# Dealing out the last row-maximum tiles: a fixed five in every projection stretch, the rest in the first three blocks of the last visits

## The chip, the cores and the metric

The kernel runs on one core of one Trainium2 chip. The metric is device time in microseconds (us), lower is better. Before the change the median of three runs is 1620.94 us (1620.45 to 1621.42).

## The reference, cut to what matters

```python
# x: (1, 2048, 640); 32 heads of 20; one key and one value head shared by all query heads
g = sigmoid((x * gate_w).sum(-1, keepdims=True))
q = (x @ wq) -> (1, 32, 2048, 20);  k = x @ wk;  v = x @ wv
p = softmax(einsum("bhqd,bkd->bhqk", q, k) * 20 ** -0.5)
a = einsum("bhqk,bkd->bhqd", p, v) -> (1, 2048, 640) @ wo
h = layernorm(B_x)                                  # over the 640 channels
u = gelu(einsum("bsd,sf->bdf", h, w1) + b1)         # token mixing, F = 1728
b = einsum("bdf,fs->bds", u, w2) + b2, transposed back
out = g * a + (1 - g) * b
```

Everything is float32. The softmax is exact: each row of scores has its own maximum subtracted.

## The kernel before, in words

**Units and visits.** The attention is cut into 32 units (`NU`): 4 blocks of 512 queries times 8 groups of 4 heads. A unit is visited 16 times, once for every block of 128 keys, so there are 512 visits. For one visit TensorE makes 4 score tiles (128 keys by 512 queries, one head each; `qk`, L703), ScalarE turns each into `p` with one exponential (L712), and `pv_group` (L738) multiplies the four `p` tiles by the values. Two visits are closed by one group of L738 instructions, which therefore marks the end of a stretch or block of work in the trace.

**Two row halves.** A score tile contracts only 62 rows. TensorE is used as two halves of 64 rows, called lane 0 and lane 1 here (`b` in the code), which work on different tiles at the same time. A score tile, a maximum tile and a 64-row projection matmul (320 columns) each take one lane. The group L738 takes all 128 rows, so both lanes have to be done before it.

**Row maxima.** The scores of a unit need its row maxima first. They come from extra tiles, the same products the other way round (128 queries by 512 keys, `ms_next`, L491), each followed by a VectorE maximum into one column of `mp` (L497): 32 tiles per lane and unit, 1024 per lane in all. When a unit has all of them, `ms_done` takes the maximum over four columns (VectorE, L512), GpSimd negates it and splits it in two (L514 to L516). `store_max` transposes it (VectorE, L523) and writes it to DRAM (`m_scr`, L524); `fetch_max` reads it back with four DMAs into rows 60, 61, 124 and 125 of the query tile `qst` (L531), two for each lane. A score of the next unit cannot start before its lane's two rows have landed. SyncE (SP) issues these DMAs in program order, like all others.

**Stretches.** The order of all engines' work is written out by hand while the program is built. The middle of the kernel is a list `ph` of 244 stretches. `main(k, ...)` issues one: one lane gets score tiles ("s") and maximum tiles ("m") after a letter pattern, the other one the projection matmuls ("F") and a few tiles; then come the last steps of the stretch and a group L738 for two visits. A small clock (`issue`, `bank_take`, `bank_give`, with 0.232 us for a tile and 0.147 us for an F) decides which lane issues next, and which of the PSUM banks in `pool` a tile gets. `later` is a list of small steps that close an earlier unit; `settle` takes one or two of them at fixed places.

The last 32 stretches (`4 * NA`, k from 212 to 243) are the **projection stretches**: their F are 15 matmuls by `wo` (L949) for the first 8 tiles of tokens. Their pattern holds 4 "m" for one lane and 1 for the other, and `share(k)` says how many of the maximum tiles still left a stretch makes. When all maxima are made, `spare[0]` becomes true, which among other things brings three more buffers for `p` into use.

**The last visits.** The last 26 visits (`TAIL`) are made in 13 **blocks** of two (`BLOCKS`, v = 486, 488, ... 510). A block has 8 score tiles, one visit ahead of the visits that it closes, and as its F the `wo` matmuls that are left (L904; `tail_take`). How many F a block gets follows from what its lane still has to do until the end (`own` and `tail`). In the loop a lane issues a score when enough banks are free by the clock, otherwise an F; then comes L738. The first score of the last unit (visit 496) stands in the block that begins at v = 494, the fifth. Behind the blocks comes an end of about 13 us with the last head group.

Of the kernel before, what the change touches and what calls it, by code (L numbers as in the profile page):

```python
# [27 lines left out]
NU = NQB * NQ  # L28
PRO = 7
LEAD = 46  # L30
TAIL = 26
BLOCKS = (2,) * 13
NA = 8
NP = 12
EPS = 1e-5
GC = math.sqrt(2.0 / math.pi)
# [4 lines left out]
def mix_kernel(ctx: ExitStack, tc: tile.TileContext, A_x, A_wq, A_wk, A_wv, A_wo,  # L41
               B_x, B_w1, B_b1, B_w2, B_b2, gate_w, out):
    nc = tc.nc
    x = A_x[0]
    y_out = out[0]

    def f32(ap):
        return ap.bitcast(F32)
# [25 lines left out]
    def view(t, at, n):  # L74
        return t[:, at:at + n * HD2].rearrange("p (a b) -> p a b", b=HD2)
# [84 lines left out]
    def new_qmax(n):  # L160
        if n < NU and n not in qmax:
            qmax[n] = load_q(n, "qmx")
# [9 lines left out]
    with tc.tile_pool(name="pa", bufs=1) as pa, \  # L172
# [18 lines left out]
        more = [w1r.tile([P, HS, P], F32, name="wr").rearrange("p (i j) f -> p i (j f)", i=2) for _ in range(3)]  # L191
# [255 lines left out]
    u_lo = [view(t, FC * HD2, FC) for t in (u0, slot[0])]  # L447
    pp_pool = ctx.enter_context(tc.tile_pool(name="pp", bufs=NP))
    ev = ctx.enter_context(tc.tile_pool(name="ev", bufs=1))
# [4 lines left out]
    X_US, F_US, PV_US = 0.232, 0.147, 0.858  # L454
    USE = {"exp": ("act", 0.43, 0.477, 0.65), "max": ("dve", 0.43, 0.6, 0.735), "sum": ("dve", 0.35, 0.47, 0.6)}

    def bank_take():
        i = min(range(len(pool)), key=lambda j: pool[j][0])
        return pool.pop(i)[1]

    def bank_give(bank, use):
        engine, lag, us, held = USE[use]
        start = max(clock[engine], clock["now"] + lag)
        clock[engine] = start + us
        pool.append((start + held, bank))
        return start + held

    def busy(engine, us):
        clock[engine] = max(clock[engine], clock["now"]) + us
# [3 lines left out]
    row_max = {}  # L473
    mtiles = {}
    lead_banks = [True]
    given = [0, 0]
    issued = [0, 0]

    def ms_next(b):
        k = given[b]  # L480
        if k >= 32 * NU:
            return None
        given[b] += 1
        n, r = divmod(k, 32)
        (kq, pr), qt = divmod(r // 4, 2), r % 4

        def step():
            if n not in mtiles:
                mtiles[n] = mpool.tile([P, 16, 4], F32, name="mp")
            ms = psl.tile([P, NB], F32, name="ml") if lead_banks[0] else bank_take()  # L490
            nc.tensor.matmul(ms, qmax[n][64 * b:64 * b + 60, pr, qt * P:(qt + 1) * P],  # L491
                             kst[64 * b:64 * b + 60, kq * NB:(kq + 1) * NB], start=True, stop=True)
            if not lead_banks[0]:
                bank_give(ms, "max")
            c = (2 * b + pr) * 4 + qt
            behind, last["ins"] = last["ins"], None
            r = nc.vector.tensor_reduce(mtiles[n][:, c, kq:kq + 1], ms, axis=AX.X, op=ALU.max)  # L497
            if behind is not None:
                tc.add_manual_dep(r.ins, behind.ins.name, SYNC, reason="row tiles that share a bank")
                last["sig"] = r  # L500
            issued[b] += 1
            if min(issued) == 32 * n + 1:
                new_qmax(n + 1)

        return step

    def ms_done():
        n = len(row_max)
        if n < NU and min(issued) >= 32 * (n + 1):
            mm = mmpool.tile([P, 16], F32, name="mm")  # L510
            busy("dve", 0.14)
            nc.vector.tensor_reduce(mm, mtiles.pop(n), axis=AX.X, op=ALU.max)  # L512
            mn = mmpool.tile([P, 2, 16], F32R, name="mn")
            nc.gpsimd.tensor_scalar(mm, mm, -1.0, None, op0=ALU.mult)  # L514
            nc.gpsimd.tensor_copy(mn[:, 0, :], mm)
            nc.gpsimd.tensor_sub(mn[:, 1, :], mm, f32(mn[:, 0, :]))  # L516
            row_max[n] = mn

    def store_max(n):
        mn = row_max[n]  # L520
        mt = mpool.tile([P, 32], F32, name="mt")
        busy("dve", 0.19)
        nc.vector.transpose(mt, f32(mn).rearrange("p j c -> p (j c)"))  # L523
        nc.sync.dma_start(out=m_scr[n], in_=mt)  # L524
# [139 lines left out]
    def split_wo(c):  # L664
        wr = wos[c]
        nc.gpsimd.tensor_copy(wo_hi[:, c, :], wr)
        nc.gpsimd.tensor_sub(wo_lo[:, c, :], wr, f32(wo_hi[:, c, :]))

    units = [(n, kb) for n in range(NU) for kb in range(NS)]
    ptiles = {}  # L670
    spare = [False]
    sc = [0, 0]
# [3 lines left out]
    def banks_at(t):  # L676
        return sum(e <= t for e, _ in pool)

    def next_p():
        turn_p[0] += spare[0]  # L680
        i = turn_p[0] % (NP + 3)
        return extra_p[i - 1] if 0 < i < 4 else pp_pool.tile([P, NB], F32, name="p")

    def s_next(b):
        j = sc[b]
        if j >= 2 * len(units):
            return None
        sc[b] += 1

        def step():  # L690
            qk(j // 2, j % 2, b)

        step.score = True
        return step
# [160 lines left out]
    HEAD = (H - 4) * DH  # L855
    jobs = [(st, 0, D) for st in range(NA, NS - 4)]
    jobs += [(st, 0, CUT) for st in range(NS - 4, NS)] + [(st, CUT, HEAD) for st in range(NS - 4, NS)]
# [126 lines left out]
    def split_last(raw):  # L984
        hi, lo = spare_row(0, F32R), spare_row(1, F32R)
        nc.gpsimd.tensor_copy(hi, raw)
        nc.gpsimd.tensor_sub(lo, raw, f32(hi))
        return hi, lo
# [40 lines left out]
    for i, (steps, rest, done) in enumerate(seq):  # L1029
        item, j = divmod(i + 1, 2)  # L1030
        rest.insert(0, lambda c=4 * (PRO + item) + 2 * j: w1_upto(c + 4))
    def stretches(seq):
        return [(rows[1 - b], rest if b else [], done if b else []) for rows, rest, done in seq for b in range(2)]

    ph = stretches(seq)
    m = len(ph)
# [6 lines left out]
    for c in range(DC):  # L1043
        ph[m + 18 + 16 * c][1].append(lambda c=c: load_wo(c))
        ph[m + 22 + 16 * c][1].append(lambda c=c: split_wo(c))
    aj = [a_jobs(st) for st in range(NA)]
    ph[-8][1].append(aj[0][0])
    ph += stretches(batches(aj, [1] * 2 * NA))
    visits = [0] + [2] * (len(ph) - 1)
    assert sum(visits) == len(units) - TAIL  # L1050
    early = NS - 4 - NA + 4
    for i in range(early):
# [15 lines left out]
    sent, back_in = {0}, {0}  # L1068
# [5 lines left out]
    def pattern(k):  # L1074
        return PATTERN[len(ph[k][0]) if visits[k] else 0]

    base = [[pattern(k)[int(k % 2 != h)].count("m") for k in range(len(ph))] for h in range(2)]

    def share(k):
        left = [32 * NU - x for x in given]  # L1080
        if k >= len(ph) - 4 * NA:
            return [(x * c[k] + sum(c[k:]) // 2) // sum(c[k:]) for x, c in zip(left, base)]
        over = [sum(c[k:]) - x for x, c in zip(left, base)]
        h = over.index(max(over))
        return [c[k] - (i == h and k % 4 == 1 and k < m and over[h] > 0) for i, c in enumerate(base)]

    lanes = [0.0, 0.0]
# [85 lines left out]
    v = 0  # L1173
    clock.update(now=0.0, act=0.0, dve=0.0, pv=0.0)
    for k in range(len(ph)):
        n = visits[k]
# [3 lines left out]
            raw = last_wo()  # L1180
        if k == len(ph) - 2:
            w_last = split_last(raw)
    assert v == len(units) - TAIL and spare[0]

    if NU - 1 not in sent:
        store_max(NU - 1)

    pool.append((lanes[0], ps_g.tile([P, NB], F32, name="g")))
    begin = lanes[0]
# [5 lines left out]
    for i in range(4):  # L1195
        tail_load(NS - 4 - NA + i, late=True)

    for n in BLOCKS:
        ends = [min(2 * len(units), 2 * (v + n) + 2) for _ in range(2)]
        lanes = [[], []]  # L1200
        own = [(2 * len(units) - c) * X_US for c in sc]
        while any(sc[b] < ends[b] for b in range(2)):
            b = int(sc[1] < sc[0])
            lanes[b].append(s_next(b))
        left = len(units) - v
        fs = [tail_take(b, len(tail[b]) if n == left else
                        max(0, round(((own[b] + len(tail[b]) * F_US) * n / left - len(lanes[b]) * X_US) / F_US)))
              for b in range(2)]
        at = [begin, begin]
        while any(lanes) or any(fs):  # L1210
            b = 0 if at[0] <= at[1] and (lanes[0] or fs[0]) or not (lanes[1] or fs[1]) else 1
            soon = sum(any(first for _, first in f[:3]) for f in fs)
            score = lanes[b] and (not fs[b] or banks_at(at[b]) > soon)
            if score or fs[b][0][1]:
                at[b] = max(at[b], min(e for e, _ in pool))
            clock["now"] = at[b]
            if score:
                lanes[b].pop(0)()
                at[b] += X_US
            else:  # L1220
                fs[b].pop(0)[0]()
                at[b] += F_US
        begin = max(at) + 0.38 + n * 0.927
        for _ in range(n):
            settle()
            pv_group([v], True)
            v += 1
        if NU - 1 not in back_in:
            fetch_max(NU - 1)
            back_in.add(NU - 1)  # L1230
        if v == 492:
            load_mid()
        if v >= 502 and len(loaded) < len(jobs):
            for i in range(len(loaded), len(jobs)):
                tail_load(i)
# [80 lines left out]
```

## Time and profile before

| | |
|---|---|
| median of three runs | 1620.94 us |
| the profiled execution, its own time | 1621.32 us |
| its span, from the first to the last instruction | 1619.5 us |
| TensorE clock granted | 1.000 |
| PE busy, share of the span | 1612.7 us, 100% |
| DVE (VectorE) busy | 1352.9 us, 84% |
| ACT (ScalarE) busy | 1309.9 us, 81% |
| POOL (GpSimd) busy | 867.9 us, 54% |
| projection stretches, from L738 to L738 | 1377.09 to 1534.32 us |
| the 13 blocks | 1534.32 to 1606.45 us |

Matmuls overlap and their ends are modelled, so a busy PE says only that some matmul was under way. Where TensorE time goes is read here from starts: from one group L738 to the next, and from one matmul to the next in its lane.

### The profile page before, as it was taken

The page shows a single profiled execution, that of the slowest core. Times are in us where ns is not written, and L with a number is a line of the kernel's source. Part 1 is how long each engine was busy: PE and PEld are TensorE (multiplying, and loading weights), DVE is VectorE, ACT ScalarE, POOL GpSimd, SP SyncE. Part 2 cuts the span into 40 slices and gives each one's busy share as a digit, 9 for nine tenths or more (in the row PEclk, how much of TensorE's full clock was granted, in tenths as well). Part 3 has the DMA queues.
Part 4 walks back from the last instruction along what each step waited for, and adds up shares of the span by engine and source line. Part 5 has one row for each costly group of instructions (what it writes and reads, how often), then busy time and mean ns, then how long its engine had stood idle before and what let it go on. Part 6 is the DMA issues. An engine that isn't in the chain of part 4 may idle for free.

```text
span 1619.5 us, 39566 instructions
## 1 busy us (share of the span) xinstructions
PE 1612.7 (100%) x14877; PEld 1126.8 (70%) x14877; DVE 1352.9 (84%) x2344; ACT 1309.9 (81%) x2567; POOL 867.9 (54%) x974
## 2 busy tenths in 40 slices
PE   9999999999999999999999999999999999999999
PEld 7789677777777777666666666666666666666666
DVE  6689999999999999888888888888888888667623
ACT  4445788888888888888888888888888888999975
POOL 6568667786777687644544444454544442344410
PEclk9999999999999999999999999999999999999999
DMA  7655323323332232232222221222222212336421
GB/s 214 210 163 147 75 68 80 86 75 87 80 85 72 79 85 65 65 72 81 72 69 76 54 73 52 65 72 80 73 72 72 69 52 60 95 111 187 149 81 43
DMA packets 188246, 144.51 MB, mean 89 GB/s; under 512 B 43474, under 2 KB 150127, under 8 KB 188055
## 3 DMA queue, kind: packets, MB, share of 16 engines
q1 hardware_dynamic: 187766, 141.66, 31.5%
q8 instruction: 117, 1.92, 0.5%
q14 instruction: 75, 0.61, 0.1%
q10 hardware_dynamic: 288, 0.33, 0.1%
HBM read 108.38 MB, written 32.15 MB: 87 GB/s over the span
## 4 chain that ended last, share of the span: by engine, by line
PE 99%; DVE 1%; ACT 0%; issue 0%; DVEq 0%; ACTq 0%
PE ms L738 16%; PE g L816 11%; PE s L738 10%; PE ms L703 10%; PE g L1004 9%; PE s L703 8%; PE s L491 7%; PE ms L491 6%; PE pp L299 4%; PE pu L624 3%; PE o L703 3%; PE o L738 3%; PE o L491 2%; PE g L949 2%; PE ml L491 1%; PE ms L904 1%
## 5 line engine op out<-in xcount | busy, mean ns | idle before, releaser
L497 DVE TENSOR_REDUCE mp<-s 128x1 f32<-128x512 f32 x895 | 586.4, 680 | 68.1 <-PE s L491 56.7
L712 ACT ACTIVATE p<-ms 128x512 f32<-128x512 f32 x938 | 545.3, 617 | 47.3 <-PE s L738 16.8
L497 DVE TENSOR_REDUCE mp<-ms 128x1 f32<-128x512 f32 x763 | 503.3, 680 | 69.5 <-PE ms L491 58.6
L751 POOL TENSOR_TENSOR acc<-acc,part 128x512 f32<-128x512 f32 x212 | 274.1, 1293 | 444.6 <-ACT part L750 432.8
L712 ACT ACTIVATE p<-s 128x512 f32<-128x512 f32 x818 | 480.2, 616 | 33.2 <-PE ms L738 10.7
L703 PE MATMUL ms<-qst,kst 62*128 62x512 f32 x938 | 366.5, 409 | 0.1
L491 PE MATMUL s<-kst,qmx 60*128 60x512 f32 x895 | 358.6, 415 | 0.6 <-DVE yo L547 0.5
L703 PE MATMUL s<-qst,kst 62*128 62x512 f32 x818 | 322.4, 409 | 0.2 <-ACT p L712 0.2
L1004 PE MATMUL g<-slot,wh 64*128 64x320 f32 x1344 | 306.0, 312 | 0.0
L491 PE MATMUL ms<-kst,qmx 60*128 60x512 f32 x763 | 302.4, 411 | 0.0
L738 PE MATMUL ms<-p,v_sb 128*32 128x512 f32 x2272 | 273.2, 598 | 0.0
L1004 PEld LDWEIGHTS g<-slot,wh 64*128 64x128 f32 x1344 | 216.6, 184 | 68.7 <-issue 54.5
L130 POOL TENSOR_TENSOR wl<-wr,wh 128x512 fp32r<-128x512 f32 (+1 forms) x176 | 217.9, 1238 | 29.6 <-ACT wh L127 12.7
L497 DVE TENSOR_REDUCE mp<-o 128x1 f32<-128x512 f32 x298 | 202.8, 681 | 35.2 <-PE o L491 29.0
L703 PEld LDWEIGHTS ms<-qst,kst 62*128 62x128 f32 x938 | 171.5, 185 | 61.5 <-ACT p L712 29.0
L1004 PE MATMUL g<-slot,wl 64*128 64x320 f32 x672 | 205.3, 306 | 0.0
L816 PE MATMUL g<-slot,wh 64*128 64x320 f32 x864 | 196.3, 309 | 0.0
L816 PE MATMUL g<-u,wh 64*128 64x320 f32 x864 | 196.3, 309 | 0.0
L703 PEld LDWEIGHTS s<-qst,kst 62*128 62x128 f32 x818 | 151.2, 185 | 53.7 <-ACT p L712 35.6
L712 ACT ACTIVATE p<-o 128x512 f32<-128x512 f32 x277 | 170.8, 617 | 12.5 <-PE ms L738 5.5
L738 PE MATMUL s<-p,v_sb 128*32 128x512 f32 x1424 | 171.2, 598 | 0.2 <-ACT p L712 0.2
L491 PEld LDWEIGHTS s<-kst,qmx 60*128 60x128 f32 x895 | 164.3, 185 | 5.6 <-DVE yo L547 0.7
(247 smaller groups left out, 3080.1 us busy)
## 6 DMA issues: line engine op xcount, KB each, us to landing
wr<-in_B_w_dram SPq DMA_DIRECT2D x136, 256.0 KB
qmx<-q_scr SPq DMA_DIRECT2D x192, 80.0 KB
qst<-q_scr SPq DMA_DIRECT2D x192, 80.0 KB
ot<-l_scr SPq DMA_DIRECT2D x120, 64.0 KB
y_scr<-yo SPq DMA_DIRECT2D x16, 320.0 KB
slot<-o_scr SPq DMA_DIRECT2D x16, 320.0 KB
o_scr<-ot SPq DMA_DIRECT2D x124, 40.0 KB
o_scr<-acc SPq DMA_DIRECT2D x124, 40.0 KB
```

The lines of the kernel that those rows point to most:

```text
L130: nc.gpsimd.tensor_sub(wl[:, :nv], wr[:, :nv], f32(wh[:, :nv]))
L299: nc.tensor.matmul(pp, w, t, start=first and n == 0, stop=not more and n == len(steps) - 1)
L491: nc.tensor.matmul(ms, qmax[n][64 * b:64 * b + 60, pr, qt * P:(qt + 1) * P], kst[64 * b:64 * b + 60, kq * NB:(kq + 1) * NB], start=True, s ...
L497: r = nc.vector.tensor_reduce(mtiles[n][:, c, kq:kq + 1], ms, axis=AX.X, op=ALU.max)
L624: nc.tensor.matmul(pu[r][:, :HD2], w[rows, c, :], h[rows, st, :], start=(st == 0 and k == 0), stop=(st == NS - 1 and k == 2))
L703: nc.tensor.matmul(s, kst[64 * b:64 * b + 62, kb * P:(kb + 1) * P], q[64 * b:64 * b + 62, pr, :], start=True, stop=True)
L712: e = nc.scalar.activation(p, s, AF.Exp, scale=SCALE)
L738: nc.tensor.matmul(o[32 * hh:32 * hh + 32, :], v_sb[:, kb + i, :], ptiles.pop((u, hh)), start=opened and i == 0, stop=(i == len(us) - 1) a ...
L751: nc.gpsimd.tensor_add(sums[0], sums[0], part)
L816: other_tile(half, nc.tensor.matmul(hold["p"][:, :HD2], w[r, i, :], u[d][r, fc, :], start=(hold["n"] == 1), stop=(hold["n"] == 6 * FC - 3)))
L949: other_tile(half, nc.tensor.matmul(hold["p"][:, :HD2], o[r, c, :], w[r, c, d * HD2:(d + 1) * HD2], start=(hold["n"] == 1), stop=(hold["n" ...
L1004: other_tile(half, nc.tensor.matmul(hold["p"][:, :HD2], w[r, st % HS, :], h[d][r, st, :], start=(hold["n"] == 1), stop=(hold["n"] == 6 * NS)))
```

## The change

`share` gives each projection stretch the number of its pattern, `c[k]` (4 for one lane and 1 for the other), as long as any are left, instead of a proportional part of what is left. What remains is put into the lanes of the first three blocks (`LAST_M`): each takes an equal part of it (rounded up), spread evenly between the block's scores. `own`, from which the number of F follows, counts these tiles too. `ms_done` stands behind each block, and the last unit's `store_max` and `fetch_max` stand together behind the block that makes its last maximum. `spare[0]` is set by hand where the blocks begin.

```diff
+LAST_M = 3
...
     def share(k):
         left = [32 * NU - x for x in given]
         if k >= len(ph) - 4 * NA:
-            return [(x * c[k] + sum(c[k:]) // 2) // sum(c[k:]) for x, c in zip(left, base)]
+            return [min(x, c[k]) for x, c in zip(left, base)]
...
-    assert v == len(units) - TAIL and spare[0]
-
-    if NU - 1 not in sent:
-        store_max(NU - 1)
+    assert v == len(units) - TAIL
+    spare[0] = True
...
-    for n in BLOCKS:
+    for j, n in enumerate(BLOCKS):
         ends = [min(2 * len(units), 2 * (v + n) + 2) for _ in range(2)]
         lanes = [[], []]
-        own = [(2 * len(units) - c) * X_US for c in sc]
+        own = [(2 * len(units) - c + 32 * NU - m) * X_US for c, m in zip(sc, given)]
         while any(sc[b] < ends[b] for b in range(2)):
             b = int(sc[1] < sc[0])
             lanes[b].append(s_next(b))
+        for b in range(2):
+            more = -(-(32 * NU - given[b]) // max(1, LAST_M - j))
+            for i in range(more):
+                lanes[b].insert((i + 1) * len(lanes[b]) // more, ms_next(b))
...
         begin = max(at) + 0.38 + n * 0.927
+        ms_done()
         for _ in range(n):
             settle()
             pv_group([v], True)
             v += 1
-        if NU - 1 not in back_in:
+        if NU - 1 in set(row_max) - sent:
+            store_max(NU - 1)
+            sent.add(NU - 1)
             fetch_max(NU - 1)
             back_in.add(NU - 1)
```

Line numbers of the changed kernel are higher by one up to the loop over the blocks (L491 becomes L492, L738 becomes L739).

## The prediction

> **What bounds the kernel now.** I read the chain that ended last first, because it says which engine's time can move the end.
>
> ```profile
> PE 99%; DVE 1%; ACT 0%; issue 0%; DVEq 0%; ACTq 0%
> ```
>
> TensorE carries 99% of the chain, so a change is worth what it does to the spacing of TensorE's starts. The order of instructions of the changed program shows where to look: every engine issues the same number of instructions as before, and the first one that stands elsewhere on TensorE lies in the middle of the projection stretches. So I cut the last part into windows at starts of the group L738, which closes each stretch and block: eleven stretches (k = 212 to 222), the other 21, and the 13 blocks.
>
> ```profile
> 1377.09:1429.76 52.67, 52.67 (x486) 33.67 (x485) 35.17 (x59) 51.01 (x105) 24.08 (x24) 1.00 0.33 94
> 1429.76:1534.32 104.56, 104.56 (x938) 66.43 (x937) 72.92 (x125) 99.48 (x201) 41.48 (x44) 1.00 0.53 160
> 1534.32:1606.45 72.13, 72.13 (x740) 48.90 (x739) 20.95 (x39) 52.27 (x105) 9.05 (x11) 1.00 0.18 55
> ```
>
> Columns are the window, its length, then busy time of PE, PEld, DVE, ACT and POOL, clock, DMA share and GB/s. The maximum tiles alone (line L491) in the first two windows:
>
> ```profile
> 1377.09:1429.76 52.67, 20.98 (x55) 9.29 (x55) 1.00 0.33 94
> 1429.76:1534.32 104.56, 46.36 (x118) 20.12 (x118) 1.00 0.53 160
> ```
>
> The first eleven stretches have 55 maximum tiles, five each, and take 52.67 / 11 = 4.788 us each. The next 21 have 118 = 21 x 5 + 13: thirteen of them hold a sixth tile. This is the comparison that the change needs, made by the kernel itself.
>
> **The change part by part: the stretches.** With five tiles everywhere, the 21 stretches should look like the eleven: 21 x 4.788 = 100.55 us instead of 104.56, so 4.01 us go, 0.308 us for each sixth tile. That is more than the tile's own step in its lane, which is 0.23 us here (first pair of rows), while a projection matmul F steps 0.15 us (second pair):
>
> ```profile
> 1558.37 0.39 PE L703 MATMUL o<-qst,kst 62*128 62x512 f32 x1
> 1558.60 0.39 PE L703 MATMUL g<-qst,kst 62*128 62x512 f32 x1
> ```
>
> ```profile
> 1538.96 0.31 PE L904 MATMUL g<-slot,u 64*128 64x320 f32 x1
> 1539.11 0.31 PE L904 MATMUL g<-slot,u 64*128 64x320 f32 x1
> ```
>
> The reason is in the letters: the sixth "m" is put behind the pattern, and `main` holds the last tile of the pattern's lane back until the other lane's F are gone. So it runs with the other half of the array empty, just ahead of L738.
>
> VectorE loses 13 maxima there, which is worth nothing: it is busy 72.92 of 104.56 us. The loads of the last projection job are the cover that gets thinner. They are issued here, and first used here:
>
> ```profile
> 1509.90 0.95 SPq L845 DMA_DIRECT2D slot<-o_scr  x2
> ```
>
> ```profile
> 1516.76 0.31 PE L949 MATMUL g<-slot 64*128 64x320 f32 x1
> ```
>
> They have 6.9 us. If the chain of DMAs that leads to them, from the end of an earlier unit, keeps its own pace, the five shortened stretches along it take at most 5 x 0.308 = 1.5 us from that. I cost it at nothing; should the loads take all of 6.9 us, it costs up to 1.5 us.
>
> **The blocks.** The 13 tiles come back here: 5, 4 and 4 in the first three blocks by the order of the changed program. The F matmuls they displace move to later blocks. F before, by the second count (weight loads) of each row of L904, with the length of the block ahead of it:
>
> ```profile
> 1534.32:1539.78 5.46, 3.02 (x34) 3.02 (x34) 1.00 0.26 76
> 1539.78:1545.22 5.44, 3.08 (x33) 2.96 (x32) 1.00 0.25 79
> 1545.22:1550.76 5.54, 3.18 (x35) 3.08 (x33) 1.00 0.34 87
> 1550.76:1556.18 5.42, 3.06 (x33) 2.97 (x32) 1.00 0.36 112
> 1556.18:1561.72 5.54, 3.19 (x35) 3.09 (x33) 1.00 0.35 110
> 1561.72:1567.20 5.48, 3.12 (x33) 3.02 (x32) 1.00 0.02 3
> 1567.20:1572.83 5.63, 3.20 (x35) 3.04 (x33) 1.00 0.28 89
> 1572.83:1578.42 5.59, 3.08 (x33) 2.90 (x32) 1.00 0.13 34
> 1578.42:1584.25 5.83, 3.56 (x34) 3.10 (x33) 1.00 0.37 112
> 1584.25:1589.72 5.47, 3.12 (x33) 2.97 (x32) 1.00 0.00 0
> 1589.72:1595.53 5.81, 3.38 (x36) 2.97 (x34) 1.00 0.01 3
> 1595.53:1601.01 5.48, 3.12 (x33) 2.95 (x32) 1.00 0.00 0
> 1601.01:1606.45 5.44, 3.05 (x41) 3.02 (x40) 1.00 0.02 3
> ```
>
> From the second block to the twelfth, those with 32 F (16 in a lane) average 5.48 us (six of them), those with 33 or 34 (17 in the fuller lane) 5.67 us (five). One more F in the fuller lane thus costs 0.19 us between blocks, and 0.147 us by the lane's step. In the changed order the blocks hold 27, 28, 28, 34, 34, 34, 34, 34, 35, 34, 35, 34 and 41 F. The fuller lane changes so:
>
> - First block: from 5 tiles and 15 F to 7 tiles and 12 F, 3.37 to 3.39 us by the steps (0.232 and 0.147). Second and third: to 6 tiles and 14 F, 3.45 us, from 3.28 and 3.43. Together 0.21 us.
> - Of the other ten blocks two keep their 17 F in the fuller lane, eight get one more: 8 x 0.147 = 1.18 us by steps, 8 x 0.19 = 1.52 us by the block rows.
>
> That makes 1.39 or 1.73 us. I take 1.7, since the block rows include what a fuller block really waits for. Bounds: the low one is 0.4 us, if the extra work fills holes. The rows show about 1.0 us of them: six blocks of 32 F lie together 0.36 us above 6 x 5.42, the five others 0.65 us above 5 x 5.54. The high one is 4.0 us, if each moved tile costs 0.308 us here too.
>
> VectorE has room: five maxima of some 0.6 us each and two additions of 0.55 us in a block of 5.5 us, at 20.95 of 72.13 us busy now. ScalarE's exponentials do not change in number.
>
> **The last unit's maxima come later.** Before, they were stored in the first block and needed in the fifth. Now `ms_done`, `store_max` and `fetch_max` follow each other directly behind the third block, and the fifth score of the fifth block, the first of the last unit, waits for lane 0's two rows. TensorE issues in order, so everything behind that score waits with it. The pieces of the chain, from before:
>
> ```profile
> 1534.08 1.27 DVE L497 TENSOR_REDUCE mp<-ms 128x1 f32<-128x512 f32 x2
> 1535.38 0.22 DVE L512 TENSOR_REDUCE mm<-mp 128x16 f32<-128x64 f32 x1
> 1537.28 0.21 DVE L523 STREAM_TRANSPOSE mt<-mn 128x32 f32<-128x32 f32 x1 [1.67 <-POOL mn L516]
> ```
>
> ```profile
> 1535.56 0.89 POOL L964 TENSOR_TENSOR yo<-yo,slot 128x320 f32<-128x320 f32 x1
> ...
> 1540.27 1.29 POOL L789 TENSOR_TENSOR acc<-acc,ot 128x512 f32<-128x512 f32 x1 [3.02 <-DMA ot<-l_scr]
> ```
>
> ```profile
> 1525.50 1.14 SPq L773 DMA_DIRECT2D l_scr<-acc  x4
> 1527.60 0.35 SPq L776 DMA_DIRECT2D rl<-l_scr  x1
> ...
> 1534.10 0.35 SPq L781 DMA_DIRECT2D l_scr<-rl  x1
> 1536.93 1.71 SPq L785 DMA_DIRECT2D ot<-l_scr  x4
> ...
> 1539.20 0.38 SPq L524 DMA_DIRECT2D m_scr<-mt  x1
> ...
> 1546.45 4.32 SPq L879 DMA_DIRECT2D slot<-o_scr  x8
> 1550.82 2.73 SPq L531 DMA_DIRECT2D qst<-m_scr  x4
> ```
>
> L512 to the end of L523 took 2.11 us, 0.85 of it because GpSimd still had L964; beside the third block GpSimd should be free, so 1.3 us. The store issues in 0.38 us and lands, by its nearest relatives, 0.96 us after its issue (L773 to L776) to 2.48 us after it (L781 to L785). Lane 0's two fetches issue in half of 2.73 us, and a small read lands 1.63 us after its issue (L785 to L789). With 0.1 us ahead of the store: 5.7 to 7.3 us from L512. Available: L512 began 1.06 us after its L738 (1534.32); one block of 5.54 us later comes the next L738, and the fifth score follows 2.42 us behind that (1558.60 against 1556.18). 5.54 + 2.42 - 1.06 = 6.9 us. So the chain is hidden by the fourth block, with 1.2 us to spare or 0.4 us missing. I take nothing; what replaces the cover if GpSimd is late again is a stall of up to 1.2 us.
>
> What is queued behind those waits: SP's store now stands behind the eight loads L879 and one output. These should end 3.4 us earlier than 1550.77 (eleven of the shortened stretches lie ahead of the unit that they hang on), about 1547.4, and the transpose is due about 1549.5, so they are clear. On VectorE the transpose waits for GpSimd about 1 us, with the next addition half a block away. The step `scale` of an earlier unit moves behind the last stretch, where it waits for its DMA anyway.
>
> **Sum.** -4.0 + 1.7 = -2.3 us. From the profiled execution's own 1621.32 us (span 1619.5) that is 1619.0; this execution lies 0.38 us above the median of 1620.94, so the median should be 1618.6 us. A measurement of this kernel can tell about 0.2%, 3.24 us, from no change: below 1617.70 is faster, above 1624.18 slower.
>
> **The rivals.**
>
> *The blocks swallow the tiles.* The extra work goes into the 1.0 us of holes, and the blocks grow by 0.4 to 0.7 us: -3.3 to -3.6, about 1617.5 us. For it: blocks of one size differ by up to 0.29 us. Against: the only early block with 34 F (first row) is no shorter than its neighbours, with one tile less.
>
> *A tile costs as much here as there.* 13 x 0.308 us come back, 1620.9 us. For it: fewer banks are free in the blocks, where the F sums hold two more of them. Against: the tiles are spread out, with F in the other lane.
>
> *ScalarE bounds the stretches.* It is busy 51.01 of 52.67 us. Then taking away TensorE work leaves a stretch as long, and only the 1.7 us stay: 1622.6 us. Against: the five-tile stretches, with the same eight exponentials, are shorter already. The Trainium skill, TensorEngine Tiling (Array Packing), section PSUM Bottleneck, says that tiling speeds up TensorE but not the emptying of PSUM, which may become the bottleneck. By that rule this rival would win; the two window rows, 4.788 us against 4.979 on average, speak against it.
>
> *The row maxima arrive late.* This one ends slower. From L512 to the end of the last fetch's issue it took 18.2 us before (1553.55), because SP had other work between. If it is as long again, lane 1's rows land 18.2 + 1.6 = 19.8 us after L512, about 11 us after that lane's first score, which stands 20 F behind lane 0's: 1618.6 + 11, about 1630 us. It decides once the chain to lane 0 takes over 6.9 + 2.3 = 9.2 us; over 0.2% slower needs 12.5 us. For it: SP is in order. Against: store and fetches are now neighbours, and what kept SP stands ahead of them.
>
> **How the numbers follow.** Forecast 0.54, swallowed tiles 0.22, equal price 0.12, ScalarE 0.04, late maxima 0.08. A tenth of the forecast's own chance lies beyond the 0.2% bound, so faster is 0.22 + 0.05 = 0.27, slower 0.08, the same 0.65. The range goes from 1617.2 (swallowed tiles, with 0.3 us more) to 1621.2 (equal price, with 0.3 us more) and leaves out ScalarE, late maxima and little else. The forecast's own range is 1617.6 to 1619.8: block growth of 0.7 to 1.7 us, or 1.7 with the stall of 1.2 us.
>
> **What would show it.** Stretches 223 to 243 all at 4.78 to 4.81 us, the blocks beginning 4.0 us earlier; the 13 blocks together 73.8 us; the fifth score of the fifth block 2.4 us behind its L738. Wrong would be: six-tile lengths in spite of five tiles, a block over 6 us, a gap ahead of that score with a wait for `m_scr`, or an end behind the last block other than 13.05 us.

## The result and the profile after

| | before | after |
|---|---|---|
| median | 1620.41 us (22 runs) | 1618.35 us (22 runs) |
| from | 1619.8 to 1621.42 us | 1617.78 to 1619.74 us |
| the profiled execution's span | 1619.5 us | 1616.3 us |

The changed kernel takes 0.9988 of the time before, 95% interval 0.9982 to 0.9993. That is 2.06 us less, 0.13%, inside the 0.2% that the prediction called the same. The forecast was 1618.6 us and 2.3 us less.

The chain that ended last in the changed kernel is TensorE's as before, with 1% on SyncE's queue (SPq):

```profile
PE 98%; SPq 1%; DVE 0%; ACT 0%; DMA 0%; issue 0%; DVEq 0%; ACTq 0%
```

The windows of the changed kernel, cut at the same groups (L738 is L739 now): eleven stretches, the other 21, the 13 blocks, and what lies behind them.

```profile
1376.01:1428.69 52.68, 52.68 (x485) 33.65 (x484) 35.17 (x59) 51.02 (x105) 24.09 (x24) 1.00 0.32 94
1428.69:1529.40 100.71, 100.71 (x925) 64.33 (x925) 65.59 (x112) 97.90 (x200) 41.17 (x43) 1.00 0.56 165
1529.40:1603.19 73.79, 73.79 (x753) 50.06 (x752) 29.04 (x52) 52.57 (x105) 9.45 (x11) 1.00 0.18 55
1603.19:1616.30 13.11, 9.31 (x65) 7.47 (x64) 7.16 (x17) 2.20 (x5) 2.59 (x3) 1.00 0.27 100
```

The 21 stretches lost 104.56 - 100.71 = 3.85 us, the blocks gained 73.79 - 72.13 = 1.66 us, the end 0.06 us. From the first stretch to the end that makes -2.1 us, the difference of the medians. The spans differ by more, because this execution reached the first stretch at 1376.01 and not at 1377.09 us. The instructions ahead of that point are the same in both, and another kernel with the changed stretches reached it at 1377.18 us, so this 1.08 us is one execution against another and no part of the change.

The maximum tiles alone (L492) in the 21 stretches and in the first three blocks:

```profile
1428.69:1529.40 100.71, 39.96 (x105) 17.74 (x105) 1.00 0.56 165
1529.40:1546.49 17.09, 4.42 (x13) 2.16 (x13) 1.00 0.30 88
```

105 is 21 x 5: the thirteen sixth tiles are gone, and thirteen stand in the blocks. Twenty of the 21 stretches take 4.78 to 4.81 us; one, from 1433.48, takes 4.92. The projection matmuls (L905) of the changed kernel's blocks; the second count is F, beside the block's length:

```profile
1529.40:1534.96 5.56, 2.95 (x27) 2.83 (x27) 1.00 0.32 104
1534.96:1540.58 5.62, 3.16 (x30) 2.99 (x28) 1.00 0.31 93
1540.58:1546.49 5.91, 3.56 (x30) 3.10 (x28) 1.00 0.26 69
...
1574.56:1580.33 5.77, 3.42 (x37) 3.29 (x35) 1.00 0.36 112
1580.33:1585.95 5.62, 3.27 (x35) 3.10 (x34) 1.00 0.02 5
1585.95:1591.74 5.79, 3.31 (x37) 3.18 (x35) 1.00 0.01 3
1591.74:1597.59 5.85, 3.67 (x35) 3.13 (x34) 1.00 0.00 0
```

Of the blocks shown, two with the same 34 F take 5.62 and 5.85 us. The count of F is not the only thing that sets a block's length.

The chain that brings the last unit's row maxima, in the changed kernel: VectorE's rows, then SyncE's queue, then the first score that needs them.

```profile
1547.32 0.22 DVE L513 TENSOR_REDUCE mm<-mp 128x16 f32<-128x64 f32 x1
1548.50 0.21 DVE L524 STREAM_TRANSPOSE mt<-mn 128x32 f32<-128x32 f32 x1 [0.95 <-POOL mn L517]
```

```profile
1548.73 0.34 SPq L525 DMA_DIRECT2D m_scr<-mt  x1
1550.18 2.74 SPq L532 DMA_DIRECT2D qst<-m_scr  x4
```

```profile
1554.58 0.39 PE L704 MATMUL g<-qst,kst 62*128 62x512 f32 x1
```

The score's row has no bracket: it waited for nothing. The two fetches of lane 0 were issued by 1550.18 + 2.74 / 2 = 1551.55 us; with the 1.63 us that a small read took to land, the rows were there at about 1553.2, 1.4 us ahead of the score.

### The profile page after: what moved, and what is told of

Read it like the earlier page. It is cut to its first block, busy times and chain, and to the rows that moved or that the text cites. A ratio compares the mean times of both kernels' runs of the same rounds, so it can differ in the third digit from the quotient of the medians.

```text
span 1616.3 us, 39559 instructions
## 1 busy us (share of the span) xinstructions
PE 1609.4 (100%) x14877; PEld 1125.7 (70%) x14877; DVE 1353.7 (84%) x2344; ACT 1309.0 (81%) x2567; POOL 868.7 (54%) x974
## 4 chain that ended last, share of the span: by engine, by line
PE 98%; SPq 1%; DVE 0%; ACT 0%; DMA 0%; issue 0%; DVEq 0%; ACTq 0%
PE ms L739 16%; PE g L817 11%; PE s L739 10%; PE ms L704 10%; PE g L1005 9%; PE s L704 8%; PE s L492 6%; PE ms L492 6%; PE pp L300 4%; PE o L739 4%; PE pu L625 3%; PE o L704 3%; PE o L492 2%; PE g L950 2%; PE s L905 1%; PE ml L492 1%
## 5 line engine op out<-in xcount | busy, mean ns | idle before, releaser
L498 DVE TENSOR_REDUCE mp<-s 128x1 f32<-128x512 f32 x878 | 576.8, 681 | 54.5 <-PE s L492 46.2
L498 DVE TENSOR_REDUCE mp<-ms 128x1 f32<-128x512 f32 x775 | 511.5, 681 | 78.8 <-PE ms L492 64.8
L713 ACT ACTIVATE p<-s 128x512 f32<-128x512 f32 x833 | 488.1, 617 | 34.1 <-PE ms L739 10.7
L492 PE MATMUL s<-kst,qmx 60*128 60x512 f32 x878 | 350.8, 414 | 0.6 <-DVE yo L548 0.5
L492 PE MATMUL ms<-kst,qmx 60*128 60x512 f32 x775 | 307.4, 411 | 0.0
L739 PE MATMUL ms<-p,v_sb 128*32 128x512 f32 x2208 | 265.5, 598 | 0.0
L713 ACT ACTIVATE p<-o 128x512 f32<-128x512 f32 x267 | 164.5, 616 | 11.1 <-PE ms L739 5.5
L739 PE MATMUL s<-p,v_sb 128*32 128x512 f32 x1392 | 167.4, 598 | 0.2 <-ACT p L713 0.2
L492 PEld LDWEIGHTS s<-kst,qmx 60*128 60x128 f32 x878 | 161.4, 185 | 5.0 <-DVE yo L548 0.7
```

Source lines behind the costliest of these rows:

```text
L713: e = nc.scalar.activation(p, s, AF.Exp, scale=SCALE)
L739: nc.tensor.matmul(o[32 * hh:32 * hh + 32, :], v_sb[:, kb + i, :], ptiles.pop((u, hh)), start=opened and i == 0, stop=(i == len(us) - 1) a ...
```

## The experiments

The open questions were three: what makes a sixth tile cost 0.31 us in a stretch, what the thirteen tiles cost in the blocks and why, and how near the chain of the maxima is to being late. The kernels ran on three chips. On the first (kernel before: 1620.62 us) were the stretches alone with GpSimd's filling, the sixth tile in the middle, the four blocks and the tiles moved within a block; on the second (1620.52) the stretches alone with VectorE's filling, two blocks, one block, and six, six and one; on the third (1620.28) the half tile and the slower additions. Each ratio is against the kernel before on the same chip. A difference of times from two chips can be off by a few tenths of a us.

**The stretches alone.** The tiles leave the stretches and are not made in the blocks; the maxima that are missing are filled in by GpSimd.

```diff
+                if n == NU - 1:
+                    nc.gpsimd.memset(mtiles[n], 0.0)
...
-        own = [(2 * len(units) - c + 32 * NU - m) * X_US for c, m in zip(sc, given)]
+        own = [(2 * len(units) - c) * X_US for c in sc]
...
-            more = -(-(32 * NU - given[b]) // max(1, LAST_M - j))
+            more = 0
+            given[b] = issued[b] = 32 * NU
```

> This kernel leaves the last 13 maximum tiles out (the last unit's maxima are taken over fewer keys); its stretches are those of the changed kernel, its blocks hold the F of the kernel before. If the sixth tiles alone made the stretches longer: stretches 212 to 243 take 153.4 us instead of 157.2, the blocks 72.1 us as before, in all 3.8 us less than before, so about 1616.6 us, and the 1.66 us that the blocks of the changed kernel grew by are the price of the 13 tiles there. If the order of banks, or the later switch to more buffers for p, lengthened the blocks by itself, they stay above 72.8 us and the whole gains less than 3.2 us.

It took 1618.54 us. The blocks fell back to 72.05 us, but the stretches did not reach 100.7: one of them took 6.56 us, with VectorE waiting 3.5 us for GpSimd's filling. The window of its 21 stretches, and of the one:

```profile
1428.74:1531.20 102.46, 101.07 (x926) 64.22 (x925) 65.62 (x112) 98.15 (x200) 41.34 (x44) 1.00 0.55 161
1476.76:1483.32 6.56, 5.17 (x46) 3.02 (x45) 3.07 (x6) 5.20 (x11) 1.37 (x2) 1.00 0.40 132
```

So this kernel measured its own filler. The same with the filling on VectorE:

```diff
-                    nc.gpsimd.memset(mtiles[n], 0.0)
+                    nc.vector.memset(mtiles[n], 0.0)
```

> The stretches alone once more: the last 13 maximum tiles are left out (the last unit's maxima are taken over fewer keys), and the tile of maxima is filled on VectorE instead of GpSimd, where the filling had held one stretch up to 6.55 us. If that was all that stood in the way, all stretches 212 to 243 take 4.78 to 4.92 us, 153.4 us together, the blocks 72.1 us, and the time is 3.8 us below the kernel before, 1616.8 us. If the gain of the five-tile stretches is not there as a whole, the time stays within 1 us of the changed kernel's 1618.4.

1616.81 us, 0.9977 of before (0.9968 to 0.9986). Its windows for the 21 stretches and the blocks:

```profile
1429.85:1530.60 100.75, 100.75 (x925) 64.37 (x925) 65.78 (x113) 97.91 (x200) 41.20 (x43) 1.00 0.57 165
1530.60:1602.68 72.08, 72.08 (x741) 48.85 (x740) 20.42 (x39) 52.45 (x105) 9.44 (x11) 1.00 0.19 56
```

The stretches alone are worth 3.7 us. The thirteen tiles in the blocks cost 1618.35 - 1616.81 = 1.54 us by the medians and 73.79 - 72.08 = 1.71 us by the windows, 0.12 to 0.13 us each, less than their own step in the lane (0.23 us) and well under what they cost in the stretches.

**Is it the place of the sixth tile?** The prediction said that it costs 0.31 us because it stands behind the pattern and runs alone. Here the kernel before puts it into the middle of its lane.

```diff
-            xs += "m" * (n_max[b] - xs.count("m"))
+            i = len(xs) // 2
+            xs = xs[:i] + "m" * (n_max[b] - xs.count("m")) + xs[i:]
```

> The kernel before, with the sixth maximum tile put into the middle of its pattern instead of behind it. If a sixth tile costs 0.31 us because it runs last with the other half of the array empty, the place decides: a lane of twelve tiles (12 x 0.235 us) then ends 0.15 us behind the other one, a six-tile stretch takes 4.94 us, and 13 x 0.15 = 2.0 us are won: 1618.4 us. If the lane is simply one step longer wherever the tile stands, 0.235 us remain of the 0.31: 1619.4 us. If the tile's price is that of its bank and of VectorE, nothing changes: 1620.4 us, stretches of 5.08.

1620.58 us, ratio 1.0001 (0.9992 to 1.001). A stretch of it with six tiles, and the 21:

```profile
1429.23:1434.31 5.08, 5.08 (x47) 3.24 (x46) 3.50 (x8) 4.85 (x11) 1.29 (x1) 1.00 1.00 232
1429.23:1533.80 104.57, 104.57 (x939) 66.45 (x938) 73.00 (x125) 99.50 (x201) 41.50 (x44) 1.00 0.54 160
```

Nothing moved, so the place is not the reason. Of the three outcomes expected, 5.08 us is the one for a price set by the tile's bank; a lane longer by one step and nothing else would have given 1619.4 us. The order of time in the kernel before shows more: the end of a stretch with five tiles (first three rows), and of one with six.

```profile
1429.28 0.40 PE L703 MATMUL s<-qst,kst 62*128 62x512 f32 x1
1429.37 0.45 PE L703 MATMUL ms<-qst,kst 62*128 62x512 f32 x1
1429.76 0.64 PE L738 MATMUL s<-p,v_sb 128*32 128x512 f32 x4
...
1434.08 0.39 PE L703 MATMUL ms<-qst,kst 62*128 62x512 f32 x1
1434.16 0.46 PE L703 MATMUL s<-qst,kst 62*128 62x512 f32 x1
1434.42 0.50 PE L491 MATMUL s<-kst,qmx 60*128 60x512 f32 x1
1434.84 0.64 PE L738 MATMUL o<-p,v_sb 128*32 128x512 f32 x4
```

With five, the two lanes end level: their last tiles start 0.09 us apart, and L738, which needs both halves of the array, starts 0.39 us behind the later one. With six, one lane is a tile longer. Its last tile starts 0.26 us after the other lane's last one, and L738 0.42 us behind it. That is 0.26 + 0.42 - 0.39 = 0.29 us, wherever in the lane the extra tile stands.

The last tile also starts late: 0.34 us after its lane's eleventh (1434.08), where the step is 0.23. ScalarE's exponential on a bank of the same name, and the tile's weight load (PEld), show why:

```profile
1433.73 0.63 ACT L712 ACTIVATE p<-s 128x512 f32<-128x512 f32 x1
```

```profile
1434.41 0.18 PEld L491 LDWEIGHTS s<-kst,qmx 60*128 60x128 f32 x1
```

The exponential ends at 1433.73 + 0.63 = 1434.36 us and the load starts 0.05 us behind it. It does so in all thirteen six-tile stretches, here and with the sixth tile in the middle, also where the bank is `o`, of which there is only one. So about 0.34 - 0.23 = 0.11 us of the 0.29 us is a wait for a bank that ScalarE has to empty; the rest is the longer lane.

**Does the tile's own length count?** If the longer lane has its part, a sixth tile of half the width should cost less by half a step. In the kernel before, the sixth tile covers 256 keys in place of 512.

```diff
-    def ms_next(b):
+    def ms_next(b, w=NB):
...
-            nc.tensor.matmul(ms, qmax[n][64 * b:64 * b + 60, pr, qt * P:(qt + 1) * P],
-                             kst[64 * b:64 * b + 60, kq * NB:(kq + 1) * NB], start=True, stop=True)
+            nc.tensor.matmul(ms[:, :w], qmax[n][64 * b:64 * b + 60, pr, qt * P:(qt + 1) * P],
+                             kst[64 * b:64 * b + 60, kq * NB:kq * NB + w], start=True, stop=True)
...
-            xs += "m" * (n_max[b] - xs.count("m"))
+            xs += "h" * (n_max[b] - xs.count("m"))
```

> The kernel before, with the sixth maximum tile of a stretch cut to 256 of its 512 keys (the last unit's maxima leave those keys out). If the 0.31 us are the lane's longer work with the other half of the array empty, the narrower tile saves its half step or somewhat more at its end: six-tile stretches of 4.95 to 4.98 us instead of 5.09, 1.5 us less in all, 1619.0 us. If they are a wait for a bank that the last tile has to sit out whatever its width, the stretches stay at 5.05 us or more and the time at 1620.4 us.

1618.9 us, ratio 0.9991 (0.9981 to 1.0). The window of the 21 stretches, and the end of one with a half tile:

```profile
1429.02:1532.12 103.10, 103.10 (x939) 66.46 (x938) 69.63 (x125) 99.35 (x201) 41.41 (x44) 1.00 0.54 161
```

```profile
1433.41 0.46 PE L703 MATMUL s<-qst,kst 62*128 62x512 f32 x1
1433.68 0.38 PE L491 MATMUL s<-kst,qmx 60*128 60x256 f32 x1
1433.99 0.64 PE L738 MATMUL o<-p,v_sb 128*32 128x512 f32 x4
```

104.56 - 103.10 = 1.46 us, 0.112 us for each of thirteen tiles, half the lane's step of 0.23 us. The half tile starts in the same place (0.27 us after the other lane's last) and L738 follows 0.31 us behind it in place of 0.42. So the stretch ends when the longer lane does, and the tile's own length counts there. The wait for the bank is untouched by the width: the weight loads start 0.05 us behind an exponential here too. A kernel without that wait wasn't tried.

**One more block.** Four blocks share the tiles, so the maxima are complete a block later.

```diff
-LAST_M = 3
+LAST_M = 4
```

> The changed kernel with the rest of the maxima spread over four blocks instead of three, so the chain from the last maximum to the last unit's first score begins one block (5.67 us) later. In the changed kernel that chain took from 1547.32 (maximum over four columns) to about 1553.2 (lane 0's rows, by the fetch's issue and 1.63 us), and the score at 1554.58 did not wait. If the chain is as long here, it ends at about 1558.9 against 1554.6: a stall of 4.3 us in the fifth block, 1622.5 us, slower than the kernel before. If the chain is shorter than its pieces say or the score has more room, no more than 2 us of stall: under 1620.4 us.

1624.44 us, ratio 1.0024 (1.0015 to 1.0034), some 6 us slower than with three. The chain in this kernel, by VectorE, SyncE's queue and TensorE:

```profile
1553.97 0.22 DVE L513 TENSOR_REDUCE mm<-mp 128x16 f32<-128x64 f32 x1
```

```profile
1555.39 0.35 SPq L525 DMA_DIRECT2D m_scr<-mt  x1
1556.88 2.80 SPq L532 DMA_DIRECT2D qst<-m_scr  x4
```

```profile
1559.81 0.47 PE L704 MATMUL ms<-qst,kst 62*128 62x512 f32 x1 [3.37 <-DMA qst<-m_scr]
1561.23 0.76 PE L704 MATMUL g<-qst,kst 62*128 62x512 f32 x1 [0.57 <-DMA qst<-m_scr]
```

From L513 to the score took 5.84 us, inside the 5.7 to 7.3 us of the prediction. The score was due 2.42 us behind the L739 at 1553.12 and came 4.27 us late: the late-maxima rival is real, one block further on. The fifth block is 5.94 us longer than with three (11.58 against 5.64), so some 1.7 us come on top of the 4.27. The granted clock alone can account for them: 0.19 x 2.20 + 0.48 x 2.70 = 1.7 us of full speed are missing in the windows below, from the wait on. The second lane's wait of 0.57 us lies in the same stretch, and the two aren't separated. (The granted clock stands ahead of the last two figures.)

```profile
1555.50:1559.80 4.30, 0.94 (x12) 0.66 (x9) 0.55 (x1) 2.06 (x4) 0.00 (x0) 1.00 0.04 6
1559.80:1562.00 2.20, 1.62 (x11) 1.30 (x13) 0.00 (x0) 1.08 (x2) 0.00 (x0) 0.81 0.40 152
1562.00:1564.70 2.70, 2.70 (x20) 2.42 (x18) 0.32 (x1) 1.19 (x2) 0.00 (x0) 0.52 0.00 0
```

**Two blocks, one block.** The same tiles closer together: 7 and 6 in two blocks, or 13 in one.

```diff
-LAST_M = 3
+LAST_M = 2
```

> The changed kernel with the rest of the maxima in two blocks (7 and 6 tiles). If a tile costs half a step, 0.13 us, wherever it stands, the 13 blocks together stay at 73.6 to 73.9 us: 1618.4 us. If the third block of the changed kernel is long (5.91 us) because fewer banks are free there, taking its tiles out wins 0.2 us: 1618.2 us. If VectorE sets the pace with seven maxima and two additions, 7 x 0.61 + 2 x 0.62 = 5.5 us in a block of 5.6, the first two blocks take over 6.0 us each and the time is 1619 us or more.

1619.7 us, ratio 0.9996 (0.9987 to 1.0004): 1.3 us above three blocks. That is close to the outcome expected if VectorE sets the pace. Its first two blocks:

```profile
1529.84:1535.83 5.99, 5.98 (x57) 3.83 (x56) 4.28 (x8) 5.82 (x13) 3.68 (x3) 1.00 0.36 116
1535.83:1542.54 6.71, 6.71 (x56) 4.13 (x55) 4.59 (x9) 4.07 (x9) 3.18 (x3) 1.00 0.24 63
```

But VectorE (third busy figure) is busy for only 4.28 of 5.99 and 4.59 of 6.71 us, so its load as a whole doesn't explain these lengths. What does stays open.

```diff
-LAST_M = 3
+LAST_M = 1
```

> The changed kernel with all 13 tiles in the first block. TensorE's two lanes would need 7 + 4 tiles each, no more than other blocks with their F. If half a step per tile is all, the blocks stay near 73.8 us and the time at 1618.4 us. If a moved tile's price is the bank that VectorE has to empty, the first block lasts as long as 13 maxima of 0.61 us and the additions, about 9 us, some 3 us more than 5.6, with that much less F left for later: 1619.5 to 1621.5 us.

1622.99 us, ratio 1.0017 (1.0008 to 1.0026). Its first two blocks, and the second half of the first:

```profile
1529.65:1538.63 8.98, 8.14 (x53) 3.88 (x52) 7.31 (x13) 6.09 (x13) 6.08 (x6) 1.00 0.30 96
1538.63:1545.83 7.20, 7.20 (x60) 4.17 (x59) 2.90 (x7) 3.67 (x9) 1.44 (x4) 0.76 0.37 94
1534.00:1538.63 4.63, 3.89 (x13) 1.47 (x13) 4.63 (x8) 2.79 (x6) 2.40 (x3) 1.00 0.32 113
```

In the last row VectorE is busy for all of 4.63 us, and TensorE gets 13 matmuls in. The first block took 8.98 us, the 9 us or so expected if VectorE's maxima set its length. Then the second block, which has no extra tile, took 7.20 us at a clock of 0.76, some 1.6 us more than such blocks take elsewhere; that is why the whole came out above the expected range.

With 13 tiles in three blocks, two blocks and one, a tile costs 0.12, about 0.22 and about 0.48 us (1.54, 2.9 and 6.2 us over the 1616.81 us). The last of these includes the clock's 1.6 us; without them it is about 0.35 us.

**The place within a block.** The third block has four extra tiles and takes 5.91 us, the second has four and takes 5.62. One kernel moves the tiles half a spacing forward, another gives six, six and one.

```diff
-                lanes[b].insert((i + 1) * len(lanes[b]) // more, ms_next(b))
+                lanes[b].insert((2 * i + 1) * len(lanes[b]) // (2 * more), ms_next(b))
```

> The changed kernel, with the moved tiles in the middle of equal parts of the lane instead of at their ends, so that none stands last in its block. The third block took 5.91 us, with its last maximum tile just ahead of L739. If that place costs, the third block falls to 5.6 to 5.7 us and the first and second stay at 5.5 to 5.65: 0.2 to 0.3 us less in all, 1618.1 us. If VectorE's or the banks' load sets the length, the three together stay at 17.1 us.

1618.57 us, ratio 0.9988 (0.9979 to 0.9997). The three blocks take 17.31 us in place of 17.09, the third of them:

```profile
1540.80:1546.93 6.13, 6.07 (x58) 3.75 (x56) 3.38 (x6) 4.14 (x9) 0.00 (x0) 1.00 0.26 70
```

So it isn't the tile at the end of the lane that makes the third block long.

```diff
-            more = -(-(32 * NU - given[b]) // max(1, LAST_M - j))
+            more = min(32 * NU - given[b], (3, 3, 32)[min(j, 2)])
```

> The changed kernel with 6, 6 and 1 tiles in the first three blocks instead of 5, 4 and 4. If the third block is long because its tiles wait for banks, it falls from 5.91 to about 5.6 us while the first two rise by 0.1 us each: 0.1 us less in all. If the number of tiles alone counts, the three blocks stay at 17.1 us together. Either way within 0.3 us of 1618.4.

1619.45 us, ratio 0.9993 (0.9984 to 1.0002): 1.1 us slower than the changed kernel, and my expectation of no difference was wrong. The second block, with six tiles, takes 6.04 us, and the third, with one, 5.70 in place of 5.91. So the number of tiles has a part in the third block's length; but the fifth block, which has none, takes 6.03 us:

```profile
1535.62:1541.66 6.04, 6.04 (x55) 3.94 (x54) 4.33 (x8) 4.03 (x9) 3.20 (x3) 1.00 0.28 78
1541.66:1547.36 5.70, 5.70 (x59) 3.79 (x58) 2.44 (x5) 3.91 (x9) 0.00 (x0) 1.00 0.22 62
1553.20:1559.23 6.03, 5.96 (x60) 3.94 (x58) 1.29 (x3) 4.15 (x10) 0.00 (x0) 1.00 0.42 124
```

**The order of the blocks' work.** The planner that writes the order gives VectorE's addition of an F sum 0.47 us; the trace has 0.55. Here the changed kernel plans with more.

```diff
-    USE = {"exp": ("act", 0.43, 0.477, 0.65), "max": ("dve", 0.43, 0.6, 0.735), "sum": ("dve", 0.35, 0.47, 0.6)}
+    USE = {"exp": ("act", 0.43, 0.477, 0.65), "max": ("dve", 0.43, 0.6, 0.735), "sum": ("dve", 0.35, 0.62, 0.75)}
```

> The changed kernel, with VectorE's addition of a finished sum entered in the program's clock with the 0.62 us that it takes from start to start instead of 0.47 (and its bank held 0.75 us). Only the order of tiles and F in the blocks and their banks change. If the moved tiles cost more than their half step because the clock gives out banks that VectorE has not emptied yet, the first three blocks fall from 17.1 us towards 16.7 and late blocks of 5.78 us and more towards 5.6: 0.3 to 1.0 us less, 1617.4 to 1618.1 us. If the two lanes' steps set the blocks, nothing changes: 1618.4 us.

1617.59 us, ratio 0.9983 (0.9974 to 0.9992), the lowest time of a kernel here that does all the work. The intervals of this ratio and the changed kernel's overlap, so what speaks for it over the changed kernel is the trace: the first three blocks, and the other ten.

```profile
1529.49:1546.59 17.10, 17.10 (x169) 11.33 (x168) 10.44 (x18) 13.58 (x28) 6.89 (x6) 1.00 0.32 85
1546.59:1602.59 56.00, 56.00 (x586) 38.32 (x586) 18.52 (x35) 38.98 (x78) 2.59 (x5) 1.00 0.16 47
```

The three blocks with the tiles stay at 17.10 us, where I expected a gain. The other ten, of which a gain was expected too, fall from 56.70 to 56.00 with the same work. What the edit would give the kernel before wasn't tried.

## Why the prediction was right, and where not

- **The stretches: right in size.** 3.85 us went where 4.01 were forecast; the one stretch of 4.92 us makes up most of the difference. The kernel's own stretches with five and with six tiles were the right comparison, and the kernel with the stretches alone gives 3.7 us.
- **The reason given for the 0.308 us: wrong.** The failing step is the sentence that the sixth tile costs more than its step because `main` holds it back behind the pattern. In these stretches the code doesn't hold it back: the condition in `main` asks that nothing stands behind the other lane's F, and there a score does. In the middle of the lane it costs the same. What the runs showed instead is a lane that is a tile longer, whose end L738 waits for, and a last tile that waits some 0.11 us for a bank that ScalarE empties. Half a tile saves half a step. The forecast stood because it used the measured difference and not the reason.
- **The blocks: 73.79 us against 73.8, with the parts off.** The three blocks with the tiles grew by 17.09 - 16.44 = 0.65 us where the steps gave 0.21; the other ten by 56.70 - 55.69 = 1.01 us where the prediction had 1.18 to 1.52 and took the higher. The two misses cancel, which is luck. The size of 0.19 us for one more F took the spread between blocks for the price of an F; the ten blocks lose 0.7 us with as many F in another order.
- **"VectorE has room": it held for four or five tiles a block.** With two blocks and one the price of a tile rises to about 0.22 and 0.48 us. VectorE is busy without a pause in the second half of the first block in the last case, but not with two blocks. The 0.308 us of the rival of equal price lies between the two.
- **The sign "a block over 6 us" did not come**, but the third block's 5.91 us was above all the rows of before, and what makes it longer than the second stays open: not the place of its tiles, and in part their number. The sign of 4.78 to 4.81 us for all stretches was missed by one.
- **The fetch chain: right.** 5.84 us measured with four blocks, in the 5.7 to 7.3 forecast. Here the score stood 1554.58 - 1547.32 = 7.3 us behind L513, and the rows were there some 1.4 us earlier, where 1.2 us to spare was the better bound. The score lay 2.42 us behind its L739 (1552.16), as forecast.
- **The rivals.** The blocks did not swallow the tiles: these cost 1.5 to 1.7 us. ScalarE does not bound the stretches as a whole: it is busy 97.90 of 100.71 us in shorter ones. But it has its part in the price of a sixth tile, by the bank that the tile waits for. The maxima were not late with three blocks, and were with four.

## What to carry to other kernels

Price an item by stretches that the kernel itself runs with and without it, and then test the reason apart from the size: here the size held and the reason did not. Where an instruction needs the whole array behind two lanes, an odd item cost more than its step where it made one lane longer and its last tile waited for a bank, and about half its step in the blocks, where other work was moved away to level the lanes. Work can be moved later only as far as the chain of transfers that hangs on its end is covered, and one block more turned a gain of 2 us into a loss of 4.

## What the runs showed of the hardware

A pause of TensorE can cost more than its own length. With four blocks, TensorE was busy 0.94 of 4.30 us, and then the granted clock was 0.81 over 2.20 us and 0.52 over 2.70 us. Within these it was 0.50:

```profile
1561.25:1564.50 3.25, 3.25 (x22) 3.17 (x22) 0.12 (x1) 1.34 (x3) 0.00 (x0) 0.50 0.08 29
```

At half speed the two windows hold 0.19 x 2.20 / 0.5 + 0.48 x 2.70 / 0.5 = 3.4 us. The Trainium skill, TensorE: Matmul & The Clock Gate, section What's actually happening, describes this: after at least one idle window the clock falls to half, and a window is 3.41 us long. The trace agrees on the half and on the 3.4 us; the pause itself was 3.37 us long.

The kernel with one block shows more. Its second block has 0.76 over 7.20 us, again 0.24 x 7.20 / 0.5 = 3.5 us at half:

```profile
1539.00:1542.00 3.00, 3.00 (x18) 0.53 (x10) 1.45 (x4) 0.13 (x1) 1.07 (x4) 0.50 0.41 98
```

But the second half of the first block has TensorE busy 3.89 of 4.63 us, so no pause was longer than 0.74 us. The same page, section HAM oscillation — how this bites in real kernels, speaks of pauses over about 3.4 us; here 13 matmuls scattered over 4.63 us were enough to lose the clock, though busy times of matmuls are modelled and may cover pauses within them.

The store and the fetch that depends on it are quick when nothing stands between: the 128x32 store's issue ended at 1548.73 + 0.34 = 1549.07 us and the fetch was issued at 1550.18, 1.1 us later.
